# A transformer block on one core: another buffer for one round of attention weights, a reordered front, and merged loads and first outputs

## The chip, the core and the metric

The kernel runs on one core of a Trainium2 chip. The core has a matrix engine (TensorE, PE in the profile), a vector engine (VectorE, DVE), an activation engine (ScalarE, ACT), a general engine (GpSimd, POOL) and a sync engine (SyncE, SP) that issues transfers. Each takes its instructions in the order written and waits for the others by semaphores. Results of matmuls lie in eight banks of PSUM, here one tile `banks` of 128 partitions and eight times 512 fp32 values. The metric is the device time of one execution in microseconds (us), the median of several.

## The reference

Block-causal attention over 8 batches, 8 heads, 576 positions of 64 values, and then a feed-forward net with a gate over the 4608 tokens:

```python
scores = scale * np.matmul(q, k.transpose(0, 1, 3, 2))
mask = block_i >= block_j                  # blocks of 64 positions
attn = softmax(np.where(mask, scores, -1e9))
x = (attn @ v).transpose(0, 2, 1, 3).reshape(4608, 512)
out = (np.maximum(x @ w_gate, 0.0) * (x @ w_val)) @ w_out    # 512 -> 1536 -> 512
```

Inputs and output are fp32; inside the matmuls operands are bf16.

## The kernel before

**Tiles.** The attention works in 32 rounds r: batch r // 4, and of its four pairs of heads the one r % 4. Positions of a batch are four chunks of 128 and a tail of 64. For batches 0 and 1 the main chunks go first and all tails are done later, for later batches tails go with the round. The feed-forward part works in nine tiles j of 512 tokens: the main positions of each batch, and one tile of all the tails. A tile has twelve units f, each of four gate and four value matmuls of 512 columns (line 656), a relu on ACT into `gate_sb` (line 665) and a product on DVE into `hT` (line 669). After them come four outputs of twelve matmuls (line 677), each copied by DVE to `ob` (line 687) and stored by `put`.

**One round.** `scores` (line 418) makes transposed scores, with two matmuls of 64 rows side by side on the array; `exp` (line 428) lets ACT write the weights to `attnT[r % 2]`; `corners` or `corner` (lines 498 to 502) zero the masked halves of the diagonal blocks; `head_av` (line 564) multiplies by v, whose 65th column of ones yields the sums; `normalise` (lines 511 and 512) divides on DVE into `xnat`; `to_xT_pe` (line 609) transposes that on PE, and ACT or DVE copies it to `xT`, on which the feed-forward tile works.

**PSUM.** `pair()` and `take(1)` hand out banks 0 to 5, the longest unused first; banks 6 and 7 (from `AV`) belong to the products with v. An instruction that writes a bank waits until the engine that reads the older content is done.

**Loads.** q, k, v and the weights come in fp32 into ten `stage` buffers by transfers on SP's queue, and POOL casts them to bf16. q and k are transposed on PE (`pe_mains`, line 313) for batches 0 and 1 and by transposing transfers for later ones. v of batch 1 comes packed (`v_p`, line 245) and is sorted by matmuls with a selection matrix (`sort_v`, line 263), which use 32 rows at a time; ACT and DVE copy the result to `v_bf` (line 272). The memory of `v_p` serves again as `attnE`, the weights of the tails of batches 0 and 1 (`scores_tails`, read by `tails_av`, line 530).

**Order.** The order on every engine is written out by hand from line 721 on. First comes the front: batch 0's rounds 0 to 3 alone. From line 781 on `ffn(n)` puts n feed-forward matmuls (in whole units) between the pieces of the attention. Lines 781 to 862 hold what the change touches: the rest of the weights, batch 1 (rounds 4 to 7), and the tails of batches 0 and 1. From line 864 on rounds 8 to 31 run in a loop that the change leaves alone. `junk` matmuls stand at the start and around the last transposes of the front; nothing reads their results.

Of the kernel before, what the change touches and what calls it, by code (L numbers as in the profile page):

```python
# [10 lines left out]
FP = mybir.dt.float32  # L11
# [6 lines left out]
def kernel(  # L18
# [30 lines left out]
    AV = 6  # L49
# [33 lines left out]
    zeros = consts.tile([128, 512], BF, name="zeros")  # L83
    nc.vector.memset(zeros, 0.0)

    sel = consts.tile([128, 516], BF, name="sel")
# [13 lines left out]
    def selection(eng):  # L100
        eng.memset(sel, 0.0)
        for c in range(4):
            ps = slice(32 * c, 32 * c + 32)
            eng.tensor_copy(
                sel[ps].rearrange("p (j m) -> p j m", j=4)[:, :, 0:128:4],
                ident[ps, None, 32 * c : 32 * c + 32].to_broadcast([32, 4, 32]),
            )
# [32 lines left out]
    def new_stage(w):  # L140
        return sb.tile([128, 1024], FP, name="stage", bufs=10)[:, 0:w]

    class Early:
# [112 lines left out]
        def sort_v(self, h0, engs):  # L256


            tp = [pair() for _ in range(2)]
            for j in range(4):  # L260
                for c in range(4):
                    ps = slice(32 * c, 32 * c + 32)
                    nc.tensor.matmul(
                        tp[c // 2][:, c % 2, 0:256],
                        sel[ps, 128 * j : 128 * j + 128],
                        v_p[ps, j, 64 * h0 : 64 * h0 + 256],
                        start=(j == 0),
                        stop=(j == 3),
                        skip_group_check=True,
                    )  # L270
            for i in range(2):
                engs[i](
                    v_bf[self.b % 2][:, 2 * i : 2 * i + 2, h0 : h0 + 4, 0:64],
                    tp[i][:, :, 0:256].rearrange("p g (h d) -> p g h d", d=64),
# [155 lines left out]
    def scores_1(r):  # L430

        b, hp = divmod(r, 4)
        at = attnT[r % 2]
        sc = scores(b, hp, banks[:, 0:2] if r % 2 == 0 else banks[:, 2:4], [(0, 0, True)])
        exp(at[:, :, 0:512], sc)
# [4 lines left out]
        exp(at[:, :, 512:1024], sc)  # L440

    def scores_2(r):
        b, hp = divmod(r, 4)
        sc = scores(b, hp, banks[:, 0:2] if r % 2 == 0 else banks[:, 2:4], [(0, 2, True)])
        exp(attnT[r % 2][:, :, 1024:1280], sc[:, :, 0:256])
# [55 lines left out]
    def corner(r, c, eng):  # L501
        eng.memset(attnT[r % 2][64:128, :, BASE[c] : BASE[c] + 64], 0.0)
# [46 lines left out]
    def head_av(r, hh, bank=None):  # L549
# [3 lines left out]
        at = attnT[r % 2]  # L553
# [3 lines left out]
        for p in range(blocks):  # L557
            for c in range(p + 1):
                if p == 4 and c == 4:
                    w = attnD[b % 2][:, 64 * hp : 64 * hp + 128]  # L560
                else:
                    col = BASE[c] + 128 * (p - c) if p < 4 else TAIL + 64 * c
                    w = at[:, hh, col : col + 128]
# [79 lines left out]
    def ffn_gen():  # L643

        for j in range(B + 1):
            hT = []
            x = xT_of(j) if j < B else xTt.rearrange("p h b n -> p h (b n)")
            for f in range(12):
                i, fo = f // 4, 128 * (f % 4)
                out = pair()  # L650
                steps = [(t, c) for t in range(2) for c in range(4)]
                if j < 2 and f == 0:

                    steps.sort(key=lambda tc_: tc_[1] == 3)
                for n, (t, c) in enumerate(steps):
                    nc.tensor.matmul(  # L656
                        out[:, t, :],
# [5 lines left out]
                    if (t, c) == (0, 3):  # L663
                        gate_sb = sb.tile([128, 512], BF, name="gate_sb", bufs=3)
                        nc.scalar.activation(gate_sb, out[:, 0, :], AF.Relu)  # L665
                    if n == 3:
                        yield False
                h = sb.tile([128, 512], BF, name="hT", bufs=15)
                nc.vector.tensor_tensor(  # L669
                    out=h, in0=gate_sb, in1=out[:, 1, :], op=AX.mult  # L670
                )
                hT.append(h)
                yield True
            for s, n0, n1 in outs(j):
                op = take(1)[:, 0, 0 : n1 - n0]
                for f in range(12):
                    nc.tensor.matmul(  # L677
                        op,
                        hT[f][:, 128 * s : 128 * (s + 1)],
                        wo[f // 4][:, f % 4, n0:n1],  # L680
                        start=(f == 0),
                        stop=(f == 11),
                    )
# [260 lines left out]
```

## Time and profile before

| | |
|---|---|
| median of 3 runs | 371.61 us (371.5 to 371.76) |
| the profiled execution | 371.53 us, its span 369.7 us |
| PE busy | 355.9 us (96%) |
| DVE / ACT / POOL busy | 163.2 / 172.3 / 116.5 us |
| first feed-forward matmul | 20.34 us after the span's start |
| first matmul of the first output | 47.28 us |
| first matmul of feed-forward tile 1 | 66.41 us |
| granted clock of TensorE | 1.00 throughout |

The span is the time from the first to the last instruction. In the timeline a row gives start, length, engine, line, operation, tiles and count, and in brackets how long the engine had been idle before it and what ended that. PE's matmuls are pipelined: a row of n matmuls ends about 0.16 us after the time at which the next one can be issued, and a short wait shows in brackets by that much less than it costs. The groups by line give count, busy time, the mean of one in ns, and the idle time before.

### The profile page before, as it was taken

What the parts mean: (1) busy time and instruction counts of PE and PEld (TensorE: products, weight loads), DVE (VectorE), ACT (ScalarE), POOL (GpSimd) and SP (SyncE); (2) the same over time, 40 slices, a digit from 0 to 9 for tenths busy, and PEclk for the clock granted to TensorE, in tenths of its full rate; (3) what the DMA queues carried; (4) which work ended last, traced back from release to release, by engine and by line L of the source; (5) the groups of instructions that cost most, each with busy time, mean ns of one, the idle gap of its engine ahead of it and who ended that gap; (6) DMA issues with size and microseconds to landing.
All of it is one profiled execution on the core that took longest, in us unless ns stands there. A gap on an engine that the chain in (4) does not pass through costs nothing.

```text
span 369.7 us, 7494 instructions
## 1 busy us (share of the span) xinstructions
PE 355.9 (96%) x2961; PEld 187.3 (51%) x3000; DVE 163.2 (44%) x319; ACT 172.3 (47%) x271; POOL 116.5 (31%) x163
## 2 busy tenths in 40 slices
PE   6799899999999999999999999999999999999995
PEld 3545356555555555555555555555555544444443
DVE  4634345376375543444434443444344434423422
ACT  5934656756574563465435543644364403302310
POOL 8677775156778404900391013000000000000000
PEclk9999999999999999999999999999999999999999
DMA  8999989779999979997499829072200130020013
GB/s 255 291 370 355 376 181 328 153 177 256 196 164 167 153 126 94 181 82 151 82 181 92 139 76 136 19 140 68 92 16 18 47 101 0 2 85 29 2 42 100
DMA packets 140227, 51.02 MB, mean 138 GB/s; under 512 B 119584, under 2 KB 133152, under 8 KB 140192
## 3 DMA queue, kind: packets, MB, share of 16 engines
q1 hardware_dynamic: 78528, 34.29, 39.8%
q0 software_dynamic: 56384, 7.08, 35.8%
q10 hardware_dynamic: 5280, 9.18, 7.0%
q8 instruction: 23, 0.38, 0.5%
q14 instruction: 12, 0.10, 0.1%
HBM read 37.75 MB, written 9.44 MB: 128 GB/s over the span
## 4 chain that ended last, share of the span: by engine, by line
PE 85%; DMA 9%; DVE 1%; ACT 1%; issue 1%; POOL 1%; SPq 1%; DVEq 0%; POOLq 0%
PE banks L656 46%; PE banks L677 24%; PE banks L564 7%; PE banks L418 6%; DMA stage<-in_moe_w_gate_dram 3%; DMA stage<-in_v_dram 2%; DMA qTt<-q_bt 2%; DMA stage<-in_k_dram 1%; PE banks L530 1%; SPq L156 1%; ACT attnT L428 0%; DVE hT L669 0%; ACT xT L616 0%; PE banks L609 0%; POOL v_p L245 0%
## 5 line engine op out<-in xcount | busy, mean ns | idle before, releaser
L428 ACT ACTIVATE attnT<-banks 128x1024 bf16<-128x1024 f32 (+1 forms) x124 | 89.8, 811 | 60.4 <-PE banks L418 59.7
L665 ACT ACTIVATE gate_sb<-banks 128x512 bf16<-128x512 f32 x108 | 65.2, 603 | 100.9 <-PE banks L656 100.6
L669 DVE TENSOR_TENSOR hT<-gate_sb,banks 128x512 bf16<-128x512 bf16 x108 | 74.2, 687 | 83.7 <-PE banks L656 74.1
L656 PE MATMUL banks<-xT,wg 128*128 128x512 bf16 x366 | 98.0, 379 | 1.0
L656 PE MATMUL banks<-xT,wv 128*128 128x512 bf16 x378 | 98.4, 379 | 0.3
L677 PE MATMUL banks<-wo,hT 128*128 128x512 bf16 (+1 forms) x432 | 96.1, 373 | 0.6
L656 PEld LDWEIGHTS <-wv 128*128 128x128 bf16 x432 | 42.3, 98 | 51.0
L677 PEld LDWEIGHTS <-hT 128*128 128x128 bf16 x444 | 42.3, 98 | 46.1
L656 PEld LDWEIGHTS <-wg 128*128 128x128 bf16 x432 | 40.4, 98 | 45.9 <-issue 0.8
L687 DVE COPY ob<-banks 128x512 f32<-128x512 f32 (+1 forms) x37 | 25.1, 677 | 54.0 <-PE banks L677 53.2
L361 POOL DMA_DIRECT2D v_bf<-in_v_dram x16 | 14.1, 901 | 70.1 <-PE banks L564 68.1
L564 PE MATMUL banks<-v_bf,attnT 128*128 128x65 bf16 x832 | 35.1, 194 | 1.0 <-POOL v_bf L231 0.6
L564 PEld LDWEIGHTS <-attnT 128*128 128x128 bf16 x832 | 30.6, 98 | 9.7 <-issue 1.6
L418 PE MATMUL banks<-qTm,kTm 64*128 64x512 bf16 (+3 forms) x256 | 25.0, 298 | 2.4 <-ACT attnT L428 1.4
L512 DVE TENSOR_TENSOR xnat<-banks,recip 128x640 bf16<-128x640 f32 (+2 forms) x36 | 25.9, 721 | 1.2
L418 PEld LDWEIGHTS <-kTm 64*128 64x128 bf16 x512 | 17.1, 94 | 12.4 <-issue 3.1
L511 DVE RECIPROCAL recip<-banks 128x10 f32<-128x10 f32 (+3 forms) x38 | 8.0, 210 | 30.3 <-PE banks L564 28.5
L498 DVE MEMSET attnT<- 64x192 uint32 x28 | 6.1, 218 | 23.1 <-ACT attnT L428 20.3
L361 POOL DMA_DIRECT2D q_bf<-in_q_dram x16 | 14.4, 941 | 0.0
L361 POOL DMA_DIRECT2D k_bf<-in_k_dram x16 | 14.2, 928 | 0.7 <-DMA v_bf<-in_v_dram 0.6
L656 PE MATMUL banks<-xTt,wg 128*128 128x512 bf16 x48 | 12.3, 379 | 0.1
L656 PE MATMUL banks<-xTt,wv 128*128 128x512 bf16 x46 | 12.1, 379 | 0.1
(90 smaller groups left out, 194.5 us busy)
## 6 DMA issues: line engine op xcount, KB each, us to landing
out_dram<-ob ACTq DMA_DIRECT2D x32, 256.0 KB, 2.3
stage<-in_moe_w_gate_dram SPq DMA_DIRECT2D x6, 512.0 KB, 9.4
stage<-in_moe_w_val_dram SPq DMA_DIRECT2D x6, 512.0 KB, 9.6
stage<-in_q_dram SPq DMA_DIRECT2D x6, 512.0 KB, 6.4
stage<-in_k_dram SPq DMA_DIRECT2D x6, 512.0 KB, 7.6
stage<-in_moe_w_out_dram SPq DMA_DIRECT2D x6, 512.0 KB, 9.0
stage<-in_v_dram SPq DMA_DIRECT2D x8, 256.0 KB, 6.4
q_bf<-in_q_dram POOLq DMA_DIRECT2D x16, 128.0 KB, 5.9
```

Of the source, the lines that this page charges most:

```text
L361: nc.gpsimd.dma_start(dst, src[b, :, 128 * c : 128 * c + n, :].rearrange("h p d -> p h d"),)
L418: nc.tensor.matmul(o, kTm[b % 2][ps, c, hp, :], qTm[b % 2][ps, c:4, hp, :] if main else qTt[b % 2][ps, hp, :], start=True, stop=True,)
L428: nc.scalar.activation(out, sc, AF.Exp, scale=scale)
L498: eng.memset(three[:, :, :, 0:64], 0.0)
L511: nc.vector.reciprocal(recip, av[:, :, :, 64])
L512: nc.vector.tensor_tensor(out=out, in0=av[:, :, :, 0:64], in1=recip.to_broadcast([rows, heads, n, 64]), op=AX.mult,)
L564: nc.tensor.matmul(av[:, 0, p, :], w, vb[:, c, h, :], start=(p == 0), stop=(c == p), skip_group_check=True,)
L656: nc.tensor.matmul(out[:, t, :], (wg, wv)[t][i][:, c, fo : fo + 128], x[:, c, :], start=(c == 0), stop=(c == 3),)
L665: nc.scalar.activation(gate_sb, out[:, 0, :], AF.Relu)
L669: nc.vector.tensor_tensor(out=h, in0=gate_sb, in1=out[:, 1, :], op=AX.mult)
L677: nc.tensor.matmul(op, hT[f][:, 128 * s : 128 * (s + 1)], wo[f // 4][:, f % 4, n0:n1], start=(f == 0), stop=(f == 11),)
L687: nc.vector.tensor_copy(ob, op)
```

## The change

1. Round 2 writes the weights of its first 1024 columns to `attnE` and not to `attnT[0]` (`attn(r, lo, hi)`); the other rounds stay as they were.
2. In the front the transposes of the pairs of heads, the rounds and `to_xT_pe` stand in another order; one copy to `xT` goes from ACT to DVE; the four corners of round 3 are zeroed by DVE; POOL casts the first weights earlier. The selection matrix is made by VectorE and not by GpSimd.
3. For tiles 0 and 1 the first two feed-forward units form one group: the twelve matmuls of input chunks 0 to 2 of both, and then the four of chunk 3. `ffn_parts(3)` puts the first twelve before the last transposes of the round (`to_xT_pe(3)`, `to_xT_pe(7)`). Seven junk matmuls at the front's end go.
4. The weights of units 4 to 7 are loaded in halves by columns and not by rows.
5. `sort_v` uses 64 rows at a time, one pair of banks and not two, here always the pair at `AV`. The first call moves from before unit 9 to after unit 11; the second from before round 5's products with v to after round 6's scores and `to_xT_pe(5)`, which is given bank 6.
6. The tails of batches 0 and 1 are loaded by five transfers and not ten (`Tails`), and cast after `to_xT_pe(5)`.
7. The first two outputs of tile 0 are made together, by thirds of the inner dimension. Tile 0's outputs are stored from GpSimd's queue and not from ScalarE's.
8. Between the scores of round 7 and its products with v the twelve feed-forward matmuls go; the transposes of the tails (`pe_tails`) and `to_xT_pe(6)` stand there.

```diff
+    def attn(r, lo, hi):
+        if r == 2 and hi <= 1024:
+            return attnE.rearrange("p (g n) -> p g n", g=2)[:, :, lo:hi]
+        return attnT[r % 2][:, :, lo:hi]
...
+    class Tails:
+        def load(self):
+            self.q, both = new_stage(1024)[0:64], new_stage(1024)
+            self.kv = both[:, 0:512], both[:, 512:1024]
+            nc.sync.dma_start(
+                self.q.rearrange("p (h d) -> p h d", h=16),
+                q[0:2, :, 512:576, :].rearrange("b h p d -> p (b h) d"),
+            )
+            for st, src in zip(self.kv, (k, v)):
+                for hh in range(2):
+                    nc.sync.dma_start(
+                        st[64 * hh : 64 * hh + 64].rearrange("p (h d) -> p h d", h=8),
+                        src[0:2, hh::2, 512:576, :].rearrange("b h p d -> p (b h) d"),
+                    )
...
-            tp = [pair() for _ in range(2)]
-            for j in range(4):
-                for c in range(4):
-                    ps = slice(32 * c, 32 * c + 32)
-                    nc.tensor.matmul(
-                        tp[c // 2][:, c % 2, 0:256],
-                        sel[ps, 128 * j : 128 * j + 128],
-                        v_p[ps, j, 64 * h0 : 64 * h0 + 256],
+            out = pair() if out is None else out
+            for odd in range(2):
+                for j in range(4):
+                    for g in range(2):
+                        ps = slice(64 * g, 64 * g + 64)
+                        nc.tensor.matmul(
+                            out[:, g, 256 * odd : 256 * odd + 256],
+                            sel[ps, odd, 128 * j : 128 * j + 128],
+                            v_p[ps, j, 64 * h0 : 64 * h0 + 256],
...
-            nc.scalar.dma_start(out[r0 : r0 + 128, :], ob)
+            (nc.gpsimd if j == 0 else nc.scalar).dma_start(out[r0 : r0 + 128, :], ob)
...
+            groups = [(0, 1)] if j < 2 else [(0,), (1,)]
+            groups += [(f,) for f in range(2, 12)]
+            for fs in groups:
+                out = {f: pair() for f in fs}
+                steps = [(f, t, c) for f in fs for t in range(2) for c in range(4)]
+                if len(fs) > 1:
+                    steps.sort(key=lambda step: (step[2] == 3, step[1]))
...
+            if j == 0:
+                todo = [outs(0)[0:2]] + todo[2:]
...
+    def ffn_parts(n):
+        for _ in range(n):
+            assert next(gen) is False
+            part[0] += 4
+            done[0] += 4
...
-        w_1 = load_w_in(1)
+        w_1 = [load_w_half(1, g) for g in range(2)]
...
+        scores_1(3)
+        to_xT_pe(0, (dve,), banks[:, 4])
+        e0.cast_v(6, 2, pool)
+        cast_w(w_0[0], pool)
+        head_to_xnat(2, 0)
+        head_to_xnat(2, 1)
+        scores_2(3)
+        to_xT_pe(1, (act,), banks[:, 5])
+        for c in range(4):
+            corner(3, c, nc.vector)
+        cast_w(w_0[1], pool)
+        to_xT_pe(2, (act,), banks[:, 4])
         head_to_xnat(3, 0)
         head_to_xnat(3, 1)
-        junk(5, banks[:, 0])
-        to_xT_pe(3, (act, dve), banks[:, 4])
-        junk(2, banks[:, 1])
+        taken[:] = [1, 1, 2, 2, 3, 3]
+        ffn_parts(3)
+        to_xT_pe(3, (act, dve), banks[:, 5])
...
-        ffn(32)
+        ffn(20)
...
-        ffn(32)
-        e1.pe_mains(0, (dve, act))
+        ffn(40)
+        e1.pe_mains(0, (dve, act), banks[:, AV : AV + 2])
         ffn(8)
-        e1.pe_mains(1, (act, act))
-        e1.sort_v(0, (dve, act))
-        ffn(8)
+        e1.pe_mains(1, (dve, act), banks[:, AV : AV + 2])
         scores_all(4, False)
         corners(4, nc.vector)
         ffn(16)
+        e1.sort_v(0, (dve, act), banks[:, AV : AV + 2])
         scores_all(5, False)
         corners(5, nc.vector)
         heads_av(4)
+        ffn_parts(3)
+        to_xT_pe(4, (act,))
+        ffn(12)
         ffn(12)
         e1.pe_mains(2, (dve, act))
         e1.pe_mains(3, (act, dve))
-        to_xT_pe(4, (act,))
-        ffn(12)
-        e1.sort_v(4, (dve, act))
         head_av(5, 0)
-        scores_all(6, False)
         head_av(5, 1)
         heads_to_xnat(5)
+        scores_all(6, False)
         corners(6, nc.vector)
+        to_xT_pe(5, (act,), banks[:, AV])
+        for b in range(2):
+            tails.cast(b, pool)
...
+        e1.sort_v(4, (dve, act), banks[:, AV : AV + 2])
         ffn(12)
         head_av(6, 0)
         scores_all(7, False)
...
-        ffn(12)
+        e0.pe_tails((dve, act))
+        e1.pe_tails((dve, act))
+        to_xT_pe(6, (act,))
         heads_av(7)
-        to_xT_pe(5, (act,))
-        e0.pe_tails((dve, act))
-        to_xT_pe(6, (act,))
-        e1.pe_tails((dve, act))
         scores_last(0)
+        scores_tails(0)
+        ffn_parts(3)
         to_xT_pe(7, (dve,))
-        scores_tails(0)
-        ffn(8)
...
         tails_of(x0)
         e2.transpose_tails()
+        ffn(4)
         scores_last(1)
         scores_tails(1)
         ffn(8)
         tails_to_xT(0, x0, dve)
         e2.unpermute(0, (dve, pool))
-        ffn(16)
+        ffn(8)
         e2.unpermute(1, (dve, pool))
```

More of the change, by code (lines that the diff above doesn't have):

```diff
@@ L669, in ffn_gen @@
[L669 to L672, printed above, removed]
-                yield True
[L674 to L683, printed above, removed]
-                    if f in (3, 7):
-                        yield False
-                ob = sb.tile([128, 512], FP, name="ob", bufs=3)[:, 0 : n1 - n0]
-                nc.vector.tensor_copy(ob, op)
-                if store:
-                    store.pop()()
-                store.append(lambda j=j, s=s, ob=ob, n=(n0, n1): put(j, s, ob, *n))
+                for f in fs:
+                    h = sb.tile([128, 512], BF, name="hT", bufs=15)
+                    nc.vector.tensor_tensor(
+                        out=h, in0=gate[f], in1=out[f][:, 1, :], op=AX.mult
+                    )
+                    hT.append(h)
@@ L784 @@
         e1.load_v_packed(4)
[L785 to L787 removed]
+        tails = Tails()
+        tails.load()
         e1.cast_qk(0, 4, (pool, pool))
```

154 lines of the change are left out of this document (89 added, 65 removed).

## The prediction

> **What bounds the kernel now.** I read the shares first, then PE's waits, then the timelines of PE, ACT, DVE and POOL around them.
>
> ```profile
> PE 355.9 (96%) x2961; PEld 187.3 (51%) x3000; DVE 163.2 (44%) x319; ACT 172.3 (47%) x271; POOL 116.5 (31%) x163
> ...
> L669 DVE TENSOR_TENSOR hT<-gate_sb,banks 128x512 bf16<-128x512 bf16 x108 | 74.2, 687 | 83.7 <-PE banks L656 74.1
> ```
> ```profile
> PE banks L263 <- POOL v_p L245: 1.6, 1, 1.6
> PE banks L418 <- ACT attnT L428: 1.4, 3, 0.6
> ```
>
> PE is the bound. Its work hardly changes, so the time follows from the holes in it. (The row of the products on DVE, 687 ns each, is used in E.) The one large wait behind the start is that of the sort for packed v (L263). The waits on exponentials (L418 <- ACT) lie in the front, where ACT paces:
>
> ```profile
> 6.91 4.85 ACT L428 ACTIVATE attnT<-banks 128x1024 bf16<-128x1024 f32 x6 [0.49 <-PE banks L418]
> 12.52 2.43 ACT L428 ACTIVATE attnT<-banks 128x1024 bf16<-128x1024 f32 x3 [0.76 <-POOL attnT L499]
> 14.82 0.61 ACT L616 COPY xT<-banks 128x512 bf16<-128x512 bf16 x1
> 15.28 2.48 ACT L428 ACTIVATE attnT<-banks 128x1024 bf16<-128x1024 f32 x3
> 20.11 0.37 ACT L613 COPY xT<-banks 128x256 bf16<-128x256 bf16 x1 [1.38 <-PE banks L609]
> ```
> ```profile
> 20.51 0.29 DVE L614 COPY xT<-banks 128x256 bf16<-128x256 bf16 x1 [0.90 <-ACT xT L613]
> ```
> ```profile
> 1.97 3.17 PE L716 MATMUL banks<-zeros,ident 128*128 128x512 bf16 x7 [1.97 <-POOL ident masks.py:199]
> ...
> 14.04 0.77 PE L564 MATMUL banks<-v_bf,attnT 128*128 128x65 bf16 x20
> 14.74 0.65 PE L418 MATMUL banks<-qTm,kTm 64*128 64x512 bf16 x6
> ...
> 19.67 0.40 PE L609 MATMUL banks<-ident,xnat 128*128 128x128 bf16 x4
> ...
> 20.34 0.81 PE L656 MATMUL banks<-xT,wg 128*128 128x512 bf16 x3
> ...
> 23.79 1.03 PE L656 MATMUL banks<-xT,wg 128*128 128x512 bf16 x4
> 24.66 1.03 PE L656 MATMUL banks<-xT,wv 128*128 128x512 bf16 x4
> ```
>
> A matmul of 512 columns costs PE 0.216 us here (four from 23.79 to 24.66). The sum is made against the profiled execution's 371.53 us, 0.08 below the median of 371.61.
>
> ```profile
> 18.71 1.05 POOL L407 CAST wv<-stage 128x1024 bf16<-128x1024 f32 x1
> ...
> 21.49 1.04 POOL L407 CAST wv<-stage 128x1024 bf16<-128x1024 f32 x1 [0.45 <-DMA stage<-in_moe_w_val_dram]
> ...
> 35.90 1.04 POOL L407 CAST wv<-stage 128x1024 bf16<-128x1024 f32 x1 [0.37 <-DMA stage<-in_moe_w_val_dram]
> ...
> 45.55 1.04 POOL L407 CAST wo<-stage 128x1024 bf16<-128x1024 f32 x1 [0.33 <-DMA stage<-in_moe_w_out_dram]
> ```
>
> **A, the front.** Round 2's own buffer takes away ACT's wait of 0.76 us, and the copy that goes to DVE the 0.46 between 14.82 and 15.28; what ACT now meets instead is round 3's scores, behind two heads' products on PE (0.70, 14.04 to 14.74): an estimate of 0.4, since those heads must first get their banks from DVE. The exponentials end at 17.76 - 0.76 - 0.46 + 0.4 = 16.9 and not 17.76. A corner and two heads (0.7) later the first unit starts at 17.7, and not at 20.34; seven junk matmuls go with that. Twelve matmuls (2.59) follow, then the last transposes (0.22), and now nothing stands behind them: copying began and ended 20.80 - 19.67 = 1.13 after the first of them, so PE waits 0.9 before the last four (0.86). Unit 2 starts at 22.3, 1.5 earlier than 23.79. I take -1.4, between -2.3 (no wait at the copies) and -0.7: the value weights' cast ended at 19.76 before, and if it does not move up, the value matmuls begin at 19.8 and not 19.0.
>
> The later casts are paced by transfers and stay where they are: unit 2's value weights at 22.53 (needed at 23.2), unit 10's at 36.94 (needed near 39), the last third of w_out at 46.59 (needed near 48). The selection matrix costs nothing on DVE, which was idle before its first cast; without that cover it is four copies and a memset, some 0.7. Loading in halves costs nothing while unit 6 has a margin of 1 us.
>
> The first sort on PE:
>
> ```profile
> 36.55 0.39 PE L313 MATMUL banks<-ident,k_bf 128*128 128x128 bf16 x4
> 38.49 0.62 PE L263 MATMUL banks<-v_p,sel 32*128 32x256 bf16 x16 [1.55 <-POOL v_p L245]
> 39.04 1.04 PE L656 MATMUL banks<-xT,wg 128*128 128x512 bf16 x3
> ```
>
> **B, the first sort.** PE stood between the transposes that ended near 36.77 and 38.49 (36.55 plus 0.22). Moved behind unit 11, the sort finds v_p long cast: -1.7.
>
> Sixteen matmuls of 256 columns took 0.55, four row groups at once. With 64 rows two go at once: 8 x 0.108 = 0.86, so +0.3 for each sort, between 0 and +1.2 (one at a time). Unit 10 now waits for banks that round 4's exponentials hold, +0.2. The first output starts at 47.28 - 1.4 - 1.7 + 0.5 = 44.7.
>
> Rounds 6 and 7 on PE and on ACT; feed-forward matmuls follow the scores:
>
> ```profile
> 54.63 1.02 PE L418 MATMUL banks<-qTm,kTm 64*128 64x512 bf16 x8
> 55.58 0.48 PE L564 MATMUL banks<-v_bf,attnT 128*128 128x65 bf16 x10
> ```
> ```profile
> 55.12 1.09 ACT L428 ACTIVATE attnT<-banks 128x512 bf16<-128x512 f32 x2 [0.16 <-PE banks L418]
> ...
> 56.09 1.52 ACT L428 ACTIVATE attnT<-banks 128x1024 bf16<-128x1024 f32 x2
> ...
> 59.86 2.00 ACT L428 ACTIVATE attnT<-banks 128x512 bf16<-128x512 f32 x3
> 63.63 0.59 ACT L616 COPY xT<-banks 128x512 bf16<-128x512 bf16 x1 [1.78 <-PE banks L609]
> 64.18 0.59 ACT L337 COPY kTt<-banks 128x512 bf16<-128x512 bf16 x1
> ```
>
> **C, the second sort.** It now stands behind round 6's scores and the transposes of round 5, and writes bank 6, from which ACT must first copy those transposes; that copy stands in ACT's queue behind round 6's exponentials.
>
> From the first score (54.63) to the last exponential's end (57.61) are 3.0 us, with the copy (0.59) 3.6. PE fills 0.95 with scores and 0.22 with transposes: a hole of 2.4. The sort adds 0.3, and `to_xT_pe(4)`, nearer to its normalisation than before, some 0.2: +2.9. The bounds are +1.6 (the copy goes ahead of the last two exponentials) and +3.6.
>
> Round 7 and the tails on PE:
>
> ```profile
> 58.88 0.83 PE L418 MATMUL banks<-qTm,kTm 64*128 64x512 bf16 x8
> 59.65 0.48 PE L564 MATMUL banks<-v_bf,attnT 128*128 128x65 bf16 x10
> 60.01 2.53 PE L677 MATMUL banks<-wo,hT 128*128 128x512 bf16 x11
> 62.60 0.77 PE L564 MATMUL banks<-v_bf,attnT 128*128 128x65 bf16 x20
> ...
> 66.41 0.82 PE L656 MATMUL banks<-xT,wg 128*128 128x512 bf16 x2
> ...
> 68.15 0.29 PE L530 MATMUL banks<-v_bf,v_p 128*128 128x65 bf16 x4
> ...
> 69.59 0.28 PE L470 MATMUL banks<-qTt,kTt 128*128 128x64 bf16 x4
> ```
>
> **D, round 7 and the tails.** The twelve output matmuls that hid round 7's exponentials are gone from there.
>
> The exponentials end at 61.86, 3.0 after the first score, the corners some 0.4 later. PE has 0.8 of scores, 0.4 of products, and about 0.9 of the tails' and round 6's transposes to put there: a hole of 1.3. ACT then still owes three copies (0.5 apart, 63.63 to 64.18), a short exponential and a full one, about 2.8, before unit 1 gets banks: another 0.5. Of these 1.8 the stretch from 62.60 to 66.41 has 1.0 already (3.8 for some 2.8 of work): +0.8, between 0 and +1.8.
>
> **E, the tails of batch 1.** Their scores take the banks of units 0 and 1, once DVE has made both products (0.69 each). Before, 1.44 us of `tails_av` (68.15 to 69.59) lay between; now only `scores_last` does, some 0.1. The first product comes 0.9 after unit 1's last matmul was issued (0.16 of pipeline and 0.69), the second 0.6 later, and 0.2 of scores lie between them: PE waits 0.7 and 0.4. I take +0.9, between +0.3 and +1.3.
>
> Round 12 on PE:
>
> ```profile
> 105.16 0.72 PE L418 MATMUL banks<-qTm,kTm 64*128 64x512 bf16 x8
> 106.01 0.29 PE L418 MATMUL banks<-qTt,kTm 64*128 64x64 bf16 x8
> ```
>
> **F, transfers.** At 106.01 PE waits for transposed tails that SP's queue brings; the 0.3 us is the most that lateness before it can hide.
>
> The five merged transfers carry the same bytes and their casts come before `pe_tails` needs them; GpSimd's stores sit in a queue with slack, as the buffers `ob` are wanted again much later; if not, a store's delay would hold DVE's next copy. I take nothing for either, between -0.3 and +0.5.
>
> **Sum.** -1.4 - 1.7 + 0.5 + 2.9 + 0.8 + 0.9 - 0.3 = +1.7. From the median 371.61: **373.3 us**, slower by 0.46%.
>
> **Clock.** The seven first junk matmuls took 3.17 us, 0.43 each and twice 0.216, though the granted clock reads 1.00. [...]
>
> **Rivals.**
> 1. *Not slower: hole C does not open*, because ACT gets to the copy before PE needs bank 6. For it: no row of PE before waits for a copy to xT. Against: ACT takes its instructions in order, and exponentials stand before the copy. It decides if the hole is under 0.9; without it the sum is 1.7 - 2.4 = -0.7, and as PE can't pass 106.01 before the transposed tails arrive, it gives 370.9 to 371.6. Chance 0.14.
> 2. *The front gains more, and D and E are hidden*: A at -2.3, D 0, E 0.3: 371.0. ACT and DVE have the room (47 and 44%), but not in these places. Chance 0.08.
> 3. *The clock halves after C or in the front without junk*, as it was for the first 3.17 us: half of that, 1.6, more: 374.9. For it: behind the start PE was never idle so long. Against: the holes are short against what went before. Chance 0.10.
> 4. *Weights bind the earlier front* (A at -0.7, waits at units 2 and 10): 374.2. The casts' margins of 0.7 and 2 us speak against it. Chance 0.10.
>
> **Numbers.** The forecast has 0.58; its own range is 372.3 to 374.3, from C, D and E together. A measurement here tells 0.2% (0.74 us) from no change. Faster (under 370.87): 0.10, the part of rivals 1 and 2 in which A's low end or earlier transfers come in addition. Same: 0.15, the rest of these and the forecast's low end. Slower: 0.75. The range 370.9 to 375.0 leaves out about 0.1 below and less above.
>
> **What would show it.** After: no wait of the sort for v_p; unit 0 near 17.7 and a hole of 0.9 before the fourth chunk; the second sort waiting for ACT with PE idle some 2.4 us around it; waits for ACT at `pe_tails` and for DVE at the second `scores_tails`; the loop from round 8 on as before. The prediction is wrong if PE's new waits between 44 and 74 us stay under 2 us in sum.

## The result, and the profile after

| | before | after |
|---|---|---|
| median (20 executions each) | 371.70 us | 373.08 us |
| range | 371.17 to 373.73 | 372.63 to 375.42 |
| ratio after / before | | 1.0047, 95% interval 1.0032 to 1.0062 |
| the profiled execution, its span | 371.53, 369.7 us | 374.13, 372.3 us |

The change makes the kernel slower by 1.4 us (0.37%, by the ratio 0.47%); 1.7 us had been forecast. The profiled execution of after lies 1 us above the median: its early loads came late (k of heads 2 and 3 landed at 7.45 us, and at 5.93 before), so the front is read below from another execution.

The shares of the changed kernel; PE's work is the same as before to 0.1 us:

```profile
PE 355.8 (96%) x2954; PEld 188.0 (50%) x2993; DVE 165.8 (45%) x329; ACT 170.8 (46%) x269; POOL 117.0 (31%) x161
```

PE's waits in the changed kernel (us in total, times, longest):

```profile
PE banks L301 <- ACT xT L652: 1.7, 1, 1.7
PE banks L645 <- DVE xnat L549: 1.3, 3, 0.6
...
PE banks L456 <- DVE hT L709: 0.7, 2, 0.5
PE banks L374 <- ACT attnT L466: 0.7, 2, 0.5
```

The sort's wait for `v_p` (1.6 before) is gone. In its place the sort (now L301) waits 1.7 us for ACT's copy to `xT`, transposes of heads wait for their normalisation (L645), and the tails' transposes and scores for ACT and DVE (L374, L456). The timelines of PE and of ACT there, in the changed kernel:

```profile
55.93 0.81 PE L456 MATMUL banks<-qTm,kTm 64*128 64x512 bf16 x8
57.32 0.40 PE L645 MATMUL banks<-ident,xnat 128*128 128x128 bf16 x4 [0.58 <-DVE xnat L549]
59.44 1.05 PE L301 MATMUL banks<-v_p,sel 64*128 64x256 bf16 x16 [1.72 <-ACT xT L652]
60.64 2.54 PE L724 MATMUL banks<-wo,hT 128*128 128x512 bf16 x11 [0.16 <-issue]
...
65.03 0.38 PE L374 MATMUL banks<-ident,k_bt 128*128 128x128 bf16 x4 [0.16 <-ACT attnT L466]
65.95 0.27 PE L374 MATMUL banks<-ident,q_bt 64*128 64x64 bf16 x4 [0.53 <-ACT attnT L466]
```
```profile
56.41 2.49 ACT L466 ACTIVATE attnT<-banks 128x512 bf16<-128x512 f32 x4 [0.35 <-PE banks L456]
58.76 0.62 ACT L652 COPY xT<-banks 128x512 bf16<-128x512 bf16 x1
```

This is hole C as forecast: the transposes are issued at 57.32 and ready some 0.4 later, but ACT, in order, starts their copy at 58.76, right behind round 6's four exponentials. The sort starts when the copy is done. PE is idle from 56.7 to 57.3 and from 57.7 to 59.4.

### The profile page after: what moved, and what is told of

It is laid out like the page before. It is cut to its first block, busy times and chain, and to the rows that moved or that the text cites. A ratio compares the mean times of both kernels' runs of the same rounds, so it can differ in the third digit from the quotient of the medians.

```text
span 372.3 us, 7468 instructions
## 1 busy us (share of the span) xinstructions
PE 355.8 (96%) x2954; PEld 188.0 (50%) x2993; DVE 165.8 (45%) x329; ACT 170.8 (46%) x269; POOL 117.0 (31%) x161
## 4 chain that ended last, share of the span: by engine, by line
PE 90%; ACT 4%; DMA 2%; issue 1%; DVE 1%; SPq 0%; POOL 0%; ACTq 0%
PE banks L695 50%; PE banks L724 24%; PE banks L600 7%; PE banks L456 6%; ACT attnT L466 3%; DMA stage<-in_k_dram 2%; PE banks L567 1%; PE banks L351 1%; PE banks L645 1%; PE banks L301 1%; SPq L193 0%; DVE xnat L549 0%; ACT v_p L466 0%; ACT xT L652 0%; ACT kTt L375 0%
## 5 line engine op out<-in xcount | busy, mean ns | idle before, releaser
L466 ACT ACTIVATE attnT<-banks 128x1024 bf16<-128x1024 f32 (+1 forms) x122 | 87.9, 805 | 61.3 <-PE banks L456 55.7
L456 PE MATMUL banks<-qTm,kTm 64*128 64x512 bf16 (+3 forms) x256 | 24.2, 299 | 1.1 <-ACT attnT L466 0.9
L456 PEld LDWEIGHTS <-kTm 64*128 64x128 bf16 x512 | 16.9, 94 | 11.1 <-issue 2.3
```

What stands on the lines that cost most here:

```text
L456: nc.tensor.matmul(o, kTm[b % 2][ps, c, hp, :], qTm[b % 2][ps, c:4, hp, :] if main else qTt[b % 2][ps, hp, :], start=True, stop=True,)
L466: nc.scalar.activation(out, sc, AF.Exp, scale=scale)
```

## The experiments

All times below stand against the kernel before, at 371.67 us on the same chips. Since the lines of the feed-forward issue the same weight loads in the same order in every kernel, the start of the n-th of them shows how late PE runs. I take four places: unit 2 of tile 0 (n = 17, at 23.58 us before), the first output (n = 97, 47.26), round 10 (n = 241, 97.15) and round 13 (n = 300, 116.42). The table gives, for one profiled execution each, how much later than before PE reaches the first place, and what each stretch adds; from there on nothing is added in any kernel. An entry is good to some 0.6 only: before_tails_first has the code of the kernel before up to about 96 us, and differs from it by -0.34 (its sort waits 1.2 for `v_p`, not 1.6) and by +0.59 (it waits 0.6 near 80 us for transposed tails that the kernel before has in time). So a smaller difference counts below only with the wait that makes it.

| kernel | median us | to n = 17 | 17 to 97 | 97 to 241 | 241 to 300 | sum |
|---|---|---|---|---|---|---|
| after | 373.08 | +0.01 | -1.45 | +4.63 | -0.33 | +2.86 |
| again | 374.68 | -0.61 | -1.47 | +6.25 | -0.33 | +3.84 |
| store_act | 373.80 | -1.08 | -1.47 | +6.32 | -0.34 | +3.43 |
| keep_clock | 373.32 | -1.06 | -1.47 | +4.63 | -0.33 | +1.77 |
| old_front | 375.52 | +0.41 | -1.46 | +4.78 | -0.33 | +3.40 |
| c_xt_later | 371.49 | -1.06 | -1.46 | +2.73 | +1.16 | +1.37 |
| d_units_back | 373.92 | -0.73 | -1.47 | +4.00 | -0.34 | +1.46 |
| e_tails_later | 374.02 | -1.29 | -1.47 | +4.38 | +1.18 | +2.80 |
| cde | 370.80 | -0.69 | -1.47 | +1.57 | +0.68 | +0.09 |
| cde_tails_first | 370.08 | -1.05 | -1.47 | +1.58 | -0.33 | -1.27 |
| round7_back | 369.84 | -0.90 | -1.47 | +1.10 | -0.33 | -1.60 |
| shared_buffer | 372.87 | +1.26 | -1.47 | +1.58 | -0.33 | +1.04 |
| before_tails_first | 371.19 | -0.09 | -0.34 | +0.59 | -0.28 | -0.12 |

**1. The changed kernel once more** (again)

> The changed kernel once more, for its own time beside the kernel before and a second profile. In the first profile unit 2 began at 23.80 us where 22.3 was forecast, and its early loads landed up to 1.5 us later than before's (the first k for heads 2 and 3 at 7.45 and not 5.93), after one packet of 1 KB that took 1.01 us. Theory 1 (a mishap of that one execution): here the early loads land as before, unit 2 begins near 22.4, and the profiled time is near 372.8. Rival (the change itself makes the early loads late, by GpSimd casting sooner): unit 2 begins near 23.8 again, and every execution is near 374.

374.68 us median of six (372.67 to 375.07). The early loads were in time here, n = 17 is at -0.61 (why not earlier, see A below), and the execution was slower still. So the late loads of the first profile are not what makes such executions. The times lie in two groups in both sets: of 26 executions 13 took 372.6 to 373.2 us at a mean granted clock of 0.999 to 1.0, ten took 374.3 to 375.5 at 0.991 to 0.995, and three lie near 374.2 at full clock, the profiled one with the late loads among them. Where the clock goes, the windows of this execution show (length, PE busy and count, granted clock, DMA share, GB/s):

```profile
58.50:59.00 0.50, 0.21 (x4) 1.00 1.07 412
59.00:59.50 0.50, 0.50 (x10) 0.50 1.05 395
...
62.00:62.50 0.50, 0.50 (x3) 0.58 1.17 306
62.50:63.00 0.50, 0.50 (x4) 1.00 1.36 277
```

PE's timeline of the same execution:

```profile
58.79 1.73 PE L301 MATMUL banks<-v_p,sel 64*128 64x256 bf16 x16 [1.72 <-ACT xT L652]
60.85 3.32 PE L724 MATMUL banks<-wo,hT 128*128 128x512 bf16 x11 [0.33 <-issue]
```

Behind hole C the clock is halved from 59.0 to about 62.4 us. The sort takes 1.73 and not 1.05, eleven output matmuls 3.32 and not 2.54. In the table that is 6.25 in place of 4.63: 1.6 us.

**2. Hole C undone** (c_xt_later)

```diff
         corners(6, nc.vector)
-        to_xT_pe(5, (act,), banks[:, AV])
...
         e1.sort_v(4, (dve, act), banks[:, AV : AV + 2])
         ffn(12)
+        to_xT_pe(5, (act,))
         head_av(6, 0)
```

> The changed kernel with the transposes of round 5 moved behind the twelve matmuls that follow the second sort; the sort no longer needs bank 6 copied by ACT. Theory (hole C is ACT's copy behind round 6's exponentials): PE's wait on xT at the sort (1.7 us) and the 0.6 on xnat before it go, a wait of some 0.5 on DVE for round 5's normalisation stays; 1.6 to 2.0 us faster than the changed kernel, about 0.4 under the kernel before. Rival (the time is set by transfers further on): the wait goes, and the total moves by under 0.5 us.

371.49 us (371.1 to 372.77; ratio 0.9992, 0.9979 to 1.0005), mean clock 0.998 or more in all 12 executions. The stretch from 97 to 241 falls from 4.63 to 2.73: the hole is worth 1.9. In the profiled execution part of that is lost again: a wait that the changed kernel doesn't have stands at round 12. That execution took 372.62 us, 1.1 more than the median, so most executions of this kernel can't have lost as much.

```profile
PE banks L456 <- DMA qTt<-q_bt: 1.2, 1, 1.2
```

**3. The output matmuls back into round 7** (d_units_back)

```diff
         ffn(12)
-        ffn(12)
         e1.pe_mains(2, (dve, act))
...
         e2.transpose(1)
+        ffn(12)
         e0.pe_tails((dve, act))
```

> The changed kernel with twelve output matmuls between round 7's scores and its products with v again, taken from before the transposes of heads 4 to 7 of batch 1. Theory (step D: exponentials without cover): the waits on ACT at the tails' transposes (0.16 and 0.53) and around them go, some 1.0 us faster than the changed kernel; a wait for k's cast at those earlier transposes may give 0.3 back. Rival (waits only move to the next bank): no change within 0.3 us.

373.92 us (372.62 to 374.06; ratio 1.005, 1.0033 to 1.0067). The waits for ACT at the tails' transposes (0.7 in the changed kernel) are gone from this kernel's list. The stretch falls by 0.63, to 4.00, although hole C grew (1.7 in the changed kernel's list):

```profile
PE banks L301 <- ACT xT L652: 2.0, 1, 2.0
```

Four of six executions had a mean clock of 0.993 or 0.994; the two at full clock took 372.62 and 372.68, at most 0.5 less than the changed kernel's lower group, where 1.0 had been expected.

**4. All three later edits undone** (cde): 2 and 3, and the scores of batch 1's tails behind twelve feed-forward matmuls as in 8 below.

> Both edits above, and batch 1's tail scores one unit later. Theory (the holes add up and are all that the change loses): 2.5 to 3.5 us faster than the changed kernel, so 1.0 to 2.0 us (0.3 to 0.5%) under the kernel before, which is what the front and the first sort gain. Rival (transfers for round 12 cap it, PE can't pass 106.0 us before the transposed tails land): it stays within 0.5 us of the kernel before.

370.80 us (370.25 to 374.57; ratio 0.9991, 0.9971 to 1.0011). The stretch falls to 1.57, and in the profiled execution (371.35) a transfer again takes back what is gained, now that of the other transposed tails; half of the executions took 370.25 to 370.49:

```profile
109.38 0.29 PE L507 MATMUL banks<-qTt,kTt 128*128 128x64 bf16 x4 [0.83 <-DMA kTt<-k_bt]
```

**5. The floor moved** (cde_tails_first)

```diff
                 e3.transpose(0)
-                e3.transpose(1)
                 e3.transpose_tails()
+                e3.transpose(1)
```

in the kernel of 4.

> The kernel with the three later edits undone, and in it the transposed loads of batch 3's tails issued on SyncE before the second pair of that batch's large transposes instead of behind it. Theory (a floor set by SyncE's queue: there the tails of batch 3 landed at 104.8 and 109.3 us, the tensor engine waited 0.8 us for the second, and 0.6 us that it was early came to nothing): the tails land about 3 us sooner, near 102 and 106, the wait is gone, the lead of some 0.5 us over the kernel before is kept to the end, and the time falls by 0.3 to 0.8 us, to 370.0 to 370.5. Rival (the stretch is bound by the transfers of POOL's prefetch of batch 4 that run at the same time, whatever the order on SyncE; or the large transposes, now later, make the wait for v or q of rounds 14 and 15): the time stays within 0.2 us of 370.8, and a wait for another transfer stands between 100 and 130 us.

370.08 us (369.84 to 370.65; ratio 0.9958, 0.9943 to 0.9973). The matmul that waited is issued without a wait:

```profile
108.03 0.28 PE L507 MATMUL banks<-qTt,kTt 128*128 128x64 bf16 x4
```

In these two traces the tails landed at 98.29 and 99.67 us here, and at 104.78 and 109.33 in kernel 4. The floor of step F and of the first rival is thus SP's order, and not the bytes. The spread is smaller too: seven executions within 0.8 us, twelve of cde over 4.3.

**6. The same edit in the kernel before** (before_tails_first)

> The kernel before the change with one edit: the transposed loads of batch 3's tails ahead of the second pair of large transposes on SyncE, as in the fastest kernel so far. Theory (the kernel before waits only 0.2 to 0.3 us at 106 for the transposed tails; the floor matters to a kernel that is earlier there): 0 to 0.3 us faster, 371.4 to 371.7, so that at least 1.2 us of the fastest kernel's lead over the kernel before are due to the change's front and first sort. Rival (the order of the transposes alone is the gain): 1 us or more faster, 370.1 to 370.7.

371.19 us (370.44 to 371.48; ratio 0.9976, 0.9956 to 0.9996): 0.5 faster, a little more than expected, and far from the 1.6 of kernel 5. So some 1.1 us of kernel 5's lead is the change's own: what its front and its first sort gain, less the 1.58 that it still loses from 97 to 241.

**7. The old front** (old_front): the changed kernel with the code from round 0 to the first units as before the change, round 2 in `attnT[0]`, and seven junk matmuls.

> The changed kernel with the first 24 us put back as they were before the change: round 2's exponentials in the shared buffer again, the transposes and the first feed-forward units where they stood, the evacuations on ScalarE; all later edits stay. Theory (the new front is worth 0.6 to 1.4 us to the tensor engine and the lateness behind it carries on): this kernel is slower than the changed one by 0.6 to 1.2 us, 373.7 to 374.3 on the scale of 373.1. Rival (the profiled execution of the changed kernel was right, the new front gains nothing): within 0.3 us of the changed kernel, 372.8 to 373.4. Second rival (what the new front gains is lost at a transfer, as in the kernel with the three later edits undone): also within 0.3 us, but then the trace shows unit 2 of tile 0 about 1 us later than in the changed kernel and the difference gone by 110 us, at a wait for a transfer.

375.52 us (374.28 to 376.53; ratio 1.01, 1.0078 to 1.0122). The two executions at full clock took 374.28 and 374.65, 1.2 to 2.0 more than the changed kernel's 372.6 to 373.1. In the table n = 17 comes 1.47 later than in keep_clock (part of that is the clock, see A below), and nothing of it is lost on the way. Both rivals are refuted; the theory was somewhat low.

**8. More cover for the tails of batch 1** (e_tails_later)

```diff
-        ffn(4)
+        ffn(12)
         scores_last(1)
         scores_tails(1)
-        ffn(8)
```

The expectation says "again"; before the change these scores stood behind the products of batch 0's tails, with no feed-forward between.

> The changed kernel with one edit undone: the last scores and the tails of batch 1 in round 7 come behind the 12 matmuls of the feed-forward again, not behind 4 of them. Theory (the step between the weight loads number 145 and 185 of the traces, 1.4 to 1.6 us, is this edit's): faster than the changed kernel by 0.8 to 1.6 us, 371.5 to 372.3 on the scale of 373.1. Forecast's own term: 0.9 us, bounds 0.3 to 1.3. Rival (the tensor engine waits in that stretch for ScalarE's exponentials in either order, the step is the earlier lateness carried on): within 0.3 us of the changed kernel, and the waits for the exponentials of attnT move to another line of the same round.

374.02 us (372.56 to 374.6; ratio 1.0046, 1.0027 to 1.0064), not distinguishable from the changed kernel; the executions at full clock took 372.56 to 373.21 and one, the profiled one, 374.04. The stretch falls by 0.25 only, and in this execution the transposed tails came late, as PE's list of waits says:

```profile
PE banks L456 <- DMA qTt<-q_bt: 1.3, 1, 1.3
...
PE banks L695 <- ACT v_p L466: 0.4, 2, 0.2
PE banks L456 <- DVE hT L709: 0.4, 1, 0.4
```

The rival was right that this edit is not where the time goes: of the 0.7 of waits for `hT` in the changed kernel 0.4 stays, and the units behind wait 0.2 more for exponentials.

**9. Stores by ScalarE again** (store_act)

```diff
-            (nc.gpsimd if j == 0 else nc.scalar).dma_start(out[r0 : r0 + 128, :], ob)
+            nc.scalar.dma_start(out[r0 : r0 + 128, :], ob)
```

> The changed kernel with the four stores of tile 0 issued by ScalarE again instead of POOL. The times of the changed kernel fall in two groups, near 372.9 and near 374.5. Theory (the groups are in how the chip's transfers run in that execution, not in the kernel): two groups again, the median within 0.4 us of the changed kernel. Rival (POOL's issues of 0.64 us each delay POOL's own sorting and casting, and with it what the tensor engine waits for): faster by 0.5 us or more, and one group. Second rival (ScalarE's issues of about 0.35 us each stand before the exponentials of the rounds 5 and 6, which are late already): slower by 0.3 to 1 us.

373.80 us (373.03 to 374.98), three executions at 373.03 to 373.10 with full clock and three at 374.5 to 374.98 with 0.995. Two groups as before: the queue of the stores costs or gains nothing that shows.

**10. Hole C filled** (keep_clock)

```diff
+        junk(8, banks[:, AV + 1])
         e1.sort_v(4, (dve, act), banks[:, AV : AV + 2])
```

> The changed kernel with eight matmuls of zeros (0.216 us each, 1.7 in all, into the second bank of the sort, which is free by then) put into hole C, ahead of the second sort. Theory (the times of the changed kernel fall in two groups because the idle tensor engine loses its granted clock at 58 to 63 us in about half of the executions: mean clock 0.995 and 374.3 to 375.4 us, else 0.999 to 1.0 and 372.6 to 373.1): the hole is as long as before but no longer idle, so the mean clock is 0.997 or more in every run and all times are in one group at 372.6 to 373.4. Rival (the clock falls for another reason, load or chip): two groups again, some runs at 0.995. Second rival (the matmuls outlast the hole, under 1.7 us in most executions): one group, but 0.3 to 0.8 us above 373.0.

373.32 us (372.84 to 373.53), one group, the clock 0.998 or more in all 12. PE's timeline and two windows of this kernel, at the place where the clock had been halved:

```profile
56.46 1.89 PE L772 MATMUL banks<-zeros,ident 128*128 128x512 bf16 x8
58.34 1.05 PE L301 MATMUL banks<-v_p,sel 64*128 64x256 bf16 x16
59.32 2.76 PE L724 MATMUL banks<-wo,hT 128*128 128x512 bf16 x12
```
```profile
58.00:60.00 2.00, 2.00 (x22) 1.00 1.05 389
60.00:62.00 2.00, 2.00 (x13) 1.00 1.05 381
```

The sort comes no sooner, yet no execution loses its clock: none of 12 here, ten of 26 with the hole idle. Kernel 2, without the hole, lost it in none of 12 either; the changed kernel (1) and kernel 3, with the hole and on the same chip as kernel 2, in four of six each. That the idle stretch is the cause is shown. The median lies 0.3 to 0.4 above the changed kernel's lower group, for which the trace shows no reason. (A low mean clock is not hole C's alone: the kernel before has 0.995 or less in 6 of 35 executions, at 370.95 to 375.36 us, kernel 4 in two of 12, kernel 11 in one; where, no trace here says.) This execution, with its loads in time and its clock whole, is also the best picture of the change.

**11. Round 7 in the old order** (round7_back): kernel 5 with the units of tile 1 one by one, and the tails' transposes, copies and scores where they stood before the change.

> The kernel with the three later edits undone and the tails' transposes first (370.08), and in it round 7 in the order of the kernel before: the first feed-forward units of tile 1 one by one and not merged, the tail transposes, the copies and the scores of the tails where they stood. Theory (between the weight loads 145 and 185 that kernel lost 1.3 us against the kernel before; one transposition of 0.25 is moved work, the rest are waits for banks that the merged units take two pairs at a time): most of it comes back, the time falls by 0.5 to 1.2 us, to 368.9 to 369.6. Rival (the lead is again lost at a transfer, now that of v or q of rounds 13 to 15): within 0.2 us of 370.1, and a wait for a transfer stands behind 95 us. Second rival (the merged units hide more than they cost): slower by 0.3 to 1 us.

369.84 us (369.23 to 371.07; ratio 0.9949, 0.9929 to 0.9969), the lowest median of all: 0.24 below kernel 5, whose range it overlaps, and 0.48 in the stretch. Less than expected: most of the 1.3 us that I had read between two weight loads was moved work, since the merged units start earlier (64.28 against 65.32) and stand still behind that.

**12. The shared buffer in the new front** (shared_buffer)

```diff
-        if r == 2 and hi <= 1024:
-            return attnE.rearrange("p (g n) -> p g n", g=2)[:, :, lo:hi]
```

in kernel 5. Round 2's weights are written here before round 0's products have read theirs, so those products take some of round 2's.

> The kernel with the three later edits undone and the tails' transposes first (370.08), and in it round 2's exponentials in the shared buffer again; the front's new order stays. Theory (the own buffer took away the 0.76 us that ScalarE waited in round 2 for the corner of the shared buffer; in the new order it would wait for the products of round 0's heads too): slower by 0.7 to 1.3 us, 370.8 to 371.4, and unit 2 of tile 0 as much later. Rival (the front is paced by loads and casts of k, the buffer gains nothing): within 0.2 us of 370.1.

372.87 us (372.25 to 373.0; ratio 1.0029, 1.001 to 1.0047), 2.8 above kernel 5 where I had expected 0.7 to 1.3. PE's products with v now wait for exponentials twice, and then the clock falls in the front, as the profiled execution shows; all 12 executions have a low mean clock (0.991 to 0.995). PE's timeline and windows of this kernel:

```profile
12.97 0.24 PE L598 MATMUL banks<-v_bf,attnT 128*128 128x65 bf16 x2 [0.69 <-ACT attnT L464]
13.89 0.72 PE L598 MATMUL banks<-v_bf,attnT 128*128 128x65 bf16 x18 [0.68 <-ACT attnT L464]
```
```profile
12.00:14.00 2.00, 0.63 (x10) 1.00 1.23 259
14.00:16.00 2.00, 1.70 (x40) 0.97 1.10 347
16.00:18.00 2.00, 2.00 (x23) 0.50 1.10 349
18.00:20.00 2.00, 2.00 (x29) 0.68 1.10 351
```

PE was busy 0.63 of 2 us and 1.70 of the next 2, and the clock is halved from 15.9 to 19.3. So the new order of the front needs the own buffer, and the buffer's price alone can't be read from this kernel.

## Why the prediction came right, step by step

The sum was -1.4 - 1.2 + 4.6 - 0.3 = +1.7. keep_clock's execution has -1.06 - 1.47 + 4.63 - 0.33 = +1.77 behind round 12; its span is 1.5 us longer than that of before, since behind the last output 0.26 less follows in every kernel with the change (why is open). The sum was right, and the terms in it were off by up to 0.65. That it met the measured time so closely is partly luck: A and B were off by 0.3 in opposite directions, and E, too high, made up for C and D, too low. It is luck, too, that 11 of the 20 executions lie in the lower group, so that the median does.

| step | forecast | measured | from |
|---|---|---|---|
| A, front | -1.4 | -1.06; -1.29 with a clock as in before's execution | n = 17, keep_clock and 8 |
| B, first sort | -1.2 | -1.47 | 17 to 97, in every kernel with this edit |
| C, second sort | +2.9 | +1.9 for the hole, +1.1 beside it | 2, and what stays in kernel 11 |
| D, round 7 | +0.8 | +0.63 alone; with the order of the tails 1.1 | 3 and 11 |
| E, tails of batch 1 | +0.9 | +0.25 | 8 |
| F, transfers | -0.3 | -0.33 | 241 to 300 |

2, 3 and 8 taken singly make 2.8, undone together 3.06 (4.63 - 1.57).

**A** came out 0.3 short in this execution, and by 0.1 where the clock was as before. The front of keep_clock, on PE and on ACT:

```profile
18.11 1.46 PE L695 MATMUL banks<-xT,wg 128*128 128x512 bf16 x6
...
20.70 0.39 PE L645 MATMUL banks<-ident,xnat 128*128 128x128 bf16 x4
21.87 0.59 PE L695 MATMUL banks<-xT,wg 128*128 128x512 bf16 x2 [0.79 <-DVE xT L650]
...
22.73 1.03 PE L695 MATMUL banks<-xT,wg 128*128 128x512 bf16 x4
```
```profile
7.10 4.85 ACT L466 ACTIVATE attnT<-banks 128x1024 bf16<-128x1024 f32 x6 [0.49 <-PE banks L456]
...
14.97 2.43 ACT L466 ACTIVATE attnT<-banks 128x1024 bf16<-128x1024 f32 x3 [0.60 <-PE banks L456]
```

The mechanism is the one forecast: ACT's wait of 0.76 is gone, unit 0 is at 18.1 (forecast 17.7), a hole of 0.95 at the last copies (0.9: from 20.92 to 21.87), unit 2 at 22.73 (22.3). The exponentials end at 17.4 and not at 16.9: they begin 0.19 later than before (7.10 against 6.91), and wait 0.60 for round 3's scores where 0.4 had been put. The first of these is the clock and not the change. PE's transposes of the first k start at the same time and take longer, in the kernel before and then in keep_clock:

```profile
5.36 0.44 PE L313 MATMUL banks<-ident,k_bf 128*128 128x128 bf16 x4
```
```profile
5.36 0.63 PE L351 MATMUL banks<-ident,k_bf 128*128 128x128 bf16 x4
```

Each trace's record of the granted clock begins where the clock first rises to full speed (windows before that print 1.00 all the same): two junk matmuls took 0.59 us at 5.63 in before's execution, whose record begins at 5.46, and 1.06 at 5.79 in after's, whose record begins at 6.87. It begins at 6.14 in keep_clock's, and from 4.95 to 7.80 in the other kernels with the new front. In kernel 8, where it rose at 5.37, much as before, n = 17 is at -1.29 and unit 2's first weights load at 22.29, as forecast. The selection matrix costs nothing, as forecast, though it takes more of DVE's time than the 0.7 put for it. DVE's timeline, first of keep_clock and then of the kernel before:

```profile
2.41 0.49 DVE L109 MEMSET sel<- 128x516 uint32 x1 [0.15 <-issue]
3.01 1.25 DVE L112 COPY sel<-ident 32x128 bf16<-32x128 bf16 x4
4.29 0.43 DVE L252 CAST q_bf<-stage 128x512 bf16<-128x512 f32 x1
```
```profile
4.18 0.64 DVE L215 CAST q_bf<-stage 128x512 bf16<-128x512 f32 x1 [1.72 <-DMA stage<-in_q_dram]
```

The cast starts 0.11 later, but ends at 4.72 and not at 4.82, and PE's first transposes start at 4.93 in both. The clock is also part of why old_front, with the old order, is 0.41 later than before at n = 17: it rose there at 7.82, and the exponentials begin at 7.43. Against again and kernel 4, whose clock rose at 7.80 and 7.54, old_front is later by 1.02 and 1.10. By these pairs, and by kernel 8 against the kernel before (1.29), the new order is worth 1.0 to 1.3, somewhat less than the 1.4 forecast. What the later loads of q, k and v add (they landed up to 0.4 us later than before in old_front, up to 0.3 in keep_clock) isn't settled.

**B** has the right parts with other sizes. keep_clock on PE:

```profile
38.77 1.02 PE L695 MATMUL banks<-xT,wg 128*128 128x512 bf16 x4 [0.50 <-ACT attnT L466]
...
42.32 1.05 PE L301 MATMUL banks<-v_p,sel 64*128 64x256 bf16 x16
43.20 0.71 PE L456 MATMUL banks<-qTm,kTm 64*128 64x512 bf16 x8
```

The sort takes 0.88 (43.20 - 42.32; 0.86 forecast). The wait of unit 10 is 0.5, not 0.2. What I missed is a gain: scores of the kernel before waited twice for DVE's products, here at 41.79 and again at 46.46, and these waits are gone.

```profile
41.79 0.27 PE L418 MATMUL banks<-qTm,kTm 64*128 64x256 bf16 x1 [0.20 <-DVE hT L669]
```

**C** opened as described, through the one mechanism that the first rival disputed. PE's waits there are 0.58 and 1.72, 2.3 in all where 2.4 was forecast, but undoing the hole gains 1.9: the wait of some 0.6 for DVE's normalisation stays, then at the sort. What it leaves is 1.1: with the hole undone the sort still costs 0.43 more (0.98, from 53.65 to 54.63, against 0.55), and transposes and sort wait for DVE's normalisation. PE's timeline of kernel 5 says where:

```profile
47.84 0.40 PE L645 MATMUL banks<-ident,xnat 128*128 128x128 bf16 x4 [0.32 <-DVE xnat L549]
...
53.65 1.05 PE L301 MATMUL banks<-v_p,sel 64*128 64x256 bf16 x16 [0.40 <-DVE xnat L549]
54.63 2.76 PE L724 MATMUL banks<-wo,hT 128*128 128x512 bf16 x12
```

I had 0.2 for the first of them (`to_xT_pe(4)`) and nothing for the second. So C came out at 3.0 with its terms shifted from the hole to DVE.

**D** was sized well in sum, and split wrongly: the missing output matmuls cost 0.63, the new order of the tails 0.48.

**E** was more than three times too high. The waits that I named are there but smaller (0.51 and 0.19 and not 0.7 and 0.4). PE's timeline of the changed kernel:

```profile
74.55 0.41 PE L456 MATMUL banks<-qTt,kTm 64*128 64x64 bf16 x16 [0.51 <-DVE hT L709]
75.15 0.39 PE L456 MATMUL banks<-qTt,kTm 64*128 64x64 bf16 x15 [0.19 <-DVE hT L709]
```

Moving the scores behind eight more matmuls saves 0.25 of that: in kernel 8 the first wait is gone, the second has grown to 0.37, and the unit behind waits 0.23 for exponentials.

**F** held: the kernel before had 0.3 at round 12, and the changed kernel and most of the others that are later there, or whose tails come first, gain -0.33. Kernels 2 and 8 do not, for their transposed tails came late in the profiled executions. The first rival's range without the hole, 370.9 to 371.6, has kernel 2's 371.49 in it; how much of that is the floor can't be read from the trace, whose execution lies 1.1 us above the median.

**The clock rival** had a chance of 0.10 and a price of 1.6. It happens in 10 of 26 executions, at hole C in the traces of it, at a price of 1.6 to 1.7 (6.25 and 6.32 in place of 4.63). The argument against it, that the holes are short, did not hold: with idle stretches of 0.58 and 1.72 us the clock fell in again and in store_act. The median is that of executions without it; had two more of the 20 met it, it would have been above 374.

The sign that would have refuted the forecast, new waits under 2 us in sum between 44 and 74 us, did not show: the rows of the changed kernel's timeline shown above have 0.58, 1.72, 0.16, 0.16 and 0.53 there, 3.2 in all.

## What to carry to other kernels

An in-order engine that evacuates a bank is as late as everything queued before it (PE waited 1.72 us here for a copy that stood behind 2.49 us of exponentials): ask of each bank that PE writes again which copy frees it, and what stands ahead of that copy. A gain in PE's early part is kept only up to the next transfer whose queue has its own pace (PE waited 0.83 us for it in kernel 4, and not at all in kernel 5, 0.72 faster), so move that transfer with the gain. And count PE's idle stretches against its clock: a hole of 2 us cost 1.9, and in 10 of 26 executions another 1.6.

## What was not expected of the hardware

In again's execution the granted clock fell to 0.50 for 3.41 us (59.00 to 62.42), and the longest idle stretch of PE was 1.72 us; of the 3.4 us ahead of the fall (55.6 to 59.0) PE was idle for 2.3 (0.58 and 1.72) and busy for a third. The falls in store_act (from 59.56) and in shared_buffer (from 15.87) lasted 3.41 us too. The clock first rose at 7.80 us in again, 4.95 in store_act and 5.63 in shared_buffer, with PE at work since about 1.97 in each, and it fell 51.20, 54.61 and 10.24 us later, which is 15, 16 and 3 times 3.413. In the executions of before and of after full clock is recorded for 365.23 us from the rise (5.46 and 6.87), 107 times 3.413, and 0.50 behind that. That the clock changes only at such steps from its rise is an estimate from these five executions.

If it holds, this phase would go far to explain which executions meet the fall. In steps of 3.413 us from the rise, one stretch of again (55.59 to 59.00) holds all of hole C, with PE busy for 1.12 us. In the profiled execution of after a border lies inside the hole, at 58.07; PE is busy for 2.49 us in the stretch ahead of it and 1.89 in the one behind, and the clock stays. By stretches counted so, busy for 1.12 (again) and 1.63 (store_act) the clock fell, and for 1.80 (before, at the sort's wait for `v_p`) and 1.87 (kernel 8) it did not; but for 1.91 in shared_buffer it fell, so busy time alone does not decide it.

The landing of one execution's transfers differs from another's by more than most edits are worth: k of heads 2 and 3 at 5.93 or 7.45 us, and the transposed tails of round 12, issued at 100.45 to 100.56 us, landed at 106.52 in after, 107.28 in keep_clock and 108.76 in kernel 8, which waits 1.3 us for them.
